# A fused attention and two-layer MoE kernel: ScalarE's gate moved one copy later, K and Q asked for two units ahead

## The chip, the cores and the metric

The kernel runs on one core of a Trainium2 chip. The metric is the device time of one execution in microseconds (us). The kernel before took 1169.15 us (median of 3 runs, 1167.33 to 1169.43).

## What is computed

Attention with a learned relative bias feeds two MLPs, all in float32, for 4 batches, 8 heads, 576 positions, 64 channels per head:

```python
x = (log1p(|i - j|) / log1p(max(i, 1)))[..., None]
bias = relu(x @ w1 + b1) @ w2                      # 576 x 576 for each of 8 heads
attn = softmax(q k^T / 8 + bias) @ v               # 4 x 8 x 576 x 64
x = attn.transpose(0, 2, 1, 3).reshape(2304, 512)
x = (sigmoid(x @ w_gate) * (x @ w_val)) @ w_out    # 512 -> 1536 -> 512
h = x @ w_in                                       # 512 -> 2048
out = (h * clip(h + 3, 0, 6) / 6) @ w_out2         # 2048 -> 512
```

## The kernel before, in words

**Chunks.** The query positions are cut into five chunks of 128, 128, 128, 128 and 64. A chunk's attention is made in units: one batch and one pair of heads, 16 units for a full chunk. The MLPs of a chunk run as a block of 68 steps (`STEPS`), and while block k runs, the attention of chunk k+1 is made between its steps.

**The lead** (`with ExitStack() as lead`, to line 584) makes the bias of chunk 0 and its 16 units. In turn n of its loop ScalarE takes the exponentials of unit n (L257) and the copies of unit n-1's transposes (L286), TensorE makes the product with V of unit n-2 (L302), and `att_x` splits it: ScalarE copies it to `xyh` (L321), VectorE puts the remainder into `xyl` (L322). The products with V take their PSUM banks from a pool of four, which the transposes share.

**Block 0** (`block(0)`) also prepares the weights. For each of the steps 2 to 67 SP loads the packed weight (`w_load`, L393, four buffers `wd`), `w_split` cuts it into a high and a low part (ScalarE L437, VectorE L438, L439, L442, ScalarE L447, VectorE L448, six buffers `wp`), and SP stores both parts for the later blocks (`w_store`, L453). A step is 12 products (L467): 4 slices of 128 rows, each high-high, high-low and low-high. The sum of a V step is taken out of PSUM by VectorE (L498). Early in block 0 the bias of chunk 1 is made as well, in three groups: hidden values z (ScalarE L125, VectorE L127), TensorE products (L136), ScalarE copies `bo` (L152), one store by SP (L162). Slice c of a block's input is ready when the units of head pair c have passed `att_x`; the last unit of chunk 0 is the last to do so for slice 3.

**What sets the order.** In the lead the orders of TensorE, ScalarE, VectorE and SP are written by hand. In block 0 those of TensorE and SP are; ScalarE's and VectorE's are laid out beforehand by a planner that goes by its own estimates, and each engine then works strictly in its order. Work of block 0 may be planned into the gaps of the lead, but two gates hold part of it: every SP instruction traced after the lead stands behind `gate`, every ScalarE instruction behind `gate_act` (lines 595, 596). `gate_act` is whatever `issued[1]` held at line 584: the last ScalarE instruction so recorded.

**Chunk 1's loads.** `chunk_att(1, 15.5, 67, 2)` (line 674) lays its events over block 0, one unit about every 3 steps. The event of a unit (`first`) asks for the bias rows and Q (`load_rows`, only with the first unit of a head pair) and K (`load_k`) of the next unit, then makes its own scores. K has four buffers, Q two, the bias rows two.

Of the kernel before, what the change touches and what calls it, by code (L numbers as in the profile page):

```python
# [12 lines left out]
AF = mybir.ActivationFunctionType  # L13
# [43 lines left out]
def fused_kernel(ctx: ExitStack, tc: tile.TileContext, qd, kd, vd, tz, rd, zc, w2b, iden, wpack, out):  # L57
    nc = tc.nc
# [22 lines left out]
    def mm_ps():  # L81
        return m1.tile([128, 512], F32, name="ps")
# [12 lines left out]
    t0 = S - QC[0][1]  # L95
# [10 lines left out]
    for g in (2, 3):  # L106
        nc.tensor.matmul(
            out=ps[32 * g:32 * g + 32, 0:2], lhsT=w2b_t, rhs=zc_t[:, 0:2], start=True, stop=True,
# [9 lines left out]
    def bias_hidden(G, g):  # L118

        if g == 0:  # L120
            z_q[G] = z_p.tile([128, 4, S], F32, name="z")
        t = 4 * G + g
        z, x = z_q[G][:, g], tz_t[:, S - 4 - 4 * t:2 * S - 4 - 4 * t]
        if g < 2:
            nc.scalar.activation(out=z, in_=x, func=AF.Relu, scale=sc_t[:, t:t + 1], bias=b1c)  # L125
        else:
            nc.vector.tensor_scalar(  # L127
                out=z, in0=x, scalar1=sc_t[:, t:t + 1], scalar2=zc_t[:, 2:3], op0=ALU.mult, op1=ALU.max
            )

    def bias_mm(G):
        z = z_q.pop(G)
        ps = bo_q[G] = s_ps()
        for j in range(2):
            for g in range(4):
                nc.tensor.matmul(  # L136
                    out=ps[32 * g:32 * g + 32, j, 0:NI], lhsT=w2b_t, rhs=z[:, g, NI * j:NI * j + NI],
                    start=True, stop=True, tile_position=(0, 32 * g),
                )
# [28 lines left out]
    xs, bm_q, q_q, kv_q, st, issued = {}, {}, {}, {}, {}, {}  # L168

    def bias_read(u):  # L170
        c, hp, b = u
        n = QC[c][1]
        if b == 0:
            bm = bm_p.tile([128, 2, S], F32, name="bm")
            for p in range(0, NQ, n):
                nc.sync.dma_start(out=bm[p:p + n], in_=biasD[c][:, 2 * hp:2 * hp + 2, :])
            bm_q[c, hp] = bm

    def load_rows(u, bias=True):
        c, hp, b = u  # L180
        i0, n = QC[c]
        if bias:
            bias_read(u)
        if b == 0:
            qt = q_p.tile([128, B, NQ], F32, name="qt")
            nc.sync.dma_start(out=qt[:, :, 0:n], in_=qd[hp, :, :, i0:i0 + n])
            q_q[c, hp] = qt

    def load_k(u):
        c, hp, b = u  # L190
        kts = []
        for a in range(NQ // QC[c][1]):
            kts.append(A["k"].tile([128, S], F32, name="kt"))
            nc.sync.dma_start(out=kts[a], in_=kd[b + a, hp])
        kv_q[u] = [kts, None]

    def load_v(u):
        c, hp, b = u
        vts = kv_q[u][1] = []
        for a in range(NQ // QC[c][1]):  # L200
            vts.append(A["v"].tile([128, 10, D], F32, name="vt"))
            issued[0] = nc.sync.dma_start(out=vts[a], in_=vd[b + a, hp])

    def att_load(u, bias=True):
        load_rows(u, bias)
        load_k(u)
        load_v(u)
# [14 lines left out]
    def att_qk(u):  # L222

        c, hp, b = u
        n = QC[c][1]
        kts, qt = kv_q[u][0], q_q[c, hp]
        ps = [s_ps(), s_ps()]
        for j in range(2):
            for h in range(2):
                for a, kt in enumerate(kts):  # L230
                    r = slice(64 * h, 64 * h + 64)
                    nc.tensor.matmul(  # L232
                        out=ps[h][n * a:n * a + n, j, 0:NI], lhsT=qt[r, b + a, 0:n],
                        rhs=kt[r, NI * j:NI * j + NI], start=True, stop=True, tile_position=(64 * h, n * a % 128),
                    )
        st[u] = dict(ps=ps)
# [37 lines left out]
    def att_tr(u, part, mm_ps):  # L274

        d = st[u]
        if part == 0:
            d["pt"] = pt_p.tile([128, 9, NQ], F32, name="pT")
        p = d["s"].rearrange("p h j -> p (h j)")
        ps = mm_ps()  # L280
        for t in range(3):
            k = 3 * part + t
            nc.tensor.transpose(  # L283
                out=ps[:, t * NQ:t * NQ + NQ], in_=p[:, 128 * k:128 * k + 128], identity=id_t
            )
        issued[1] = nc.scalar.activation(  # L286
            out=d["pt"][:, 3 * part:3 * part + 3],
            in_=ps[:, 0:3 * NQ].rearrange("p (t n) -> p t n", t=3), func=AF.Copy,
        )
# [17 lines left out]
    def att_x(u, po=None):  # L307

        c, hp, b = u
        n = QC[c][1]  # L310
        w = NQ if po is None else 2 * NQ
        d = st.pop(u)
        if po is None:
            po = d["po"]
        if (c, hp) not in xs:
            xs[c, hp] = (
                xy_p.tile([128, NTOK], F32R, name="xyh"),
                xy_p.tile([128, NTOK], F32R, name="xyl"),
            )
        xh, xl = (x[:, b * n:b * n + w] for x in xs[c, hp])  # L320
        nc.scalar.activation(out=xh, in_=po[:, 0:w], func=AF.Copy)  # L321
        nc.vector.tensor_tensor(out=xl, in0=po[:, 0:w], in1=xh.bitcast(F32), op=ALU.subtract)  # L322


# [54 lines left out]
    def pair_av(p):  # L379
        po = mm_ps()  # L380
        for i, u in enumerate(p):
            att_av(u, lambda: po[:, NQ * i:NQ * i + NQ])
        att_x(p[0], po)
        del st[p[1]]
# [148 lines left out]
    us = units[0]  # L533
    NL = len(us)
    NG0, NG1 = QC[0][1] // 16, 2
    with ExitStack() as lead:
        for name, bufs in (("s", 3), ("k", 6), ("v", 7), ("bo", 3), ("wf", 2), ("cv", 2)):
            A[name] = lead.enter_context(tc.tile_pool(name=name + "l", bufs=bufs))
        lead.enter_context(tc.manual_schedule(engines={ET.PE, ET.Activation, ET.DVE, ET.SP}))
        load_rows(us[0], False)  # L540
        load_k(us[0])
        nc.sync.dma_start(out=tz_t[:, 0:t0], in_=tz[:, 0:t0])
        load_k(us[1])
        load_v(us[0])
        nc.sync.dma_start(out=id_t, in_=iden)
        load_k(us[2])
        bm_q[0, 0] = bm_p.tile([128, 2, S], F32, name="bm")
        for G in range(NG0 + NG1 + 1):
            if G < NG0 + NG1:
                for g in range(4):  # L550
                    bias_hidden(G, g)
                bias_mm(G)
            if G:
                bias_out(G - 1, (G - 1) % 2, G % 2 == 0)
        for u in us[1:3]:
            load_v(u)
        att_qk(us[0])
        att_min(us[0])
        att_qk(us[1])
        for n in range(NL + 2):  # L560
            if n + 3 < NL:
                att_load(us[n + 3])
            if n in (1, 6):
                w_load(n // 6)
            if n < NL:
                att_exp(us[n])
            if n + 1 < NL:
                att_min(us[n + 1])
            if 1 <= n <= NL:
                for part in range(3):  # L570
                    att_tr(us[n - 1], part, mm_ps)
            if n < NL:
                att_norm(us[n])
            if n >= 2:
                att_av(us[n - 2], mm_ps)
                att_x(us[n - 2])
            if n + 2 < NL:
                att_qk(us[n + 2])
            if 4 <= n < 16:
                w_part((n - 4) // 6, (n - 4) % 6)  # L580
            if n == NL - 4:
                gate = issued[0]
            if n == NL - 1:
                gate_act = issued[1]

    def late(name, bufs):
# [29 lines left out]
    def chunk_att(c, t0, t1, lag):  # L616

        us = units[c]
        d = (t1 - t0) / (len(us) - 1 + lag)
        ev = [(t0 - 2 * d, lambda: att_load(us[0], False)), (t0 - d, lambda: bias_read(us[0]))]  # L620
        for i, u in enumerate(us):
            a = t0 + d * i

            def first(u=u, nxt=us[i + 1] if i + 1 < len(us) else None):
                if nxt:
                    load_rows(nxt)
                    load_k(nxt)
                att_qk(u)
                att_min(u)
                att_exp(u)  # L630
                att_norm(u)
            if i:
                ev.append((a + 0.5, lambda u=u: load_v(u)))
            for part in range(3):
                ev.append((a + lag * d - 3 + part, lambda u=u, p=part: att_tr(u, p, mm_ps)))
            ev.append((a + lag * d - 0.01, lambda u=u: (att_av(u, mm_ps), att_x(u))))
            ev.append((a, first))
        return ev
# [136 lines left out]
```

## Time and profile before

| | |
|---|---|
| median of 3 runs | 1169.15 us (1167.33 to 1169.43) |
| profiled execution, its own time | 1166.04 us |
| its span in the profile | 1164.2 us |
| TensorE busy with matmuls | 1143.6 us (98%) |
| VectorE, ScalarE busy | 631.8 us (54%), 579.7 us (50%) |
| mean granted TensorE clock | 0.996 |

The profile names engines PE (TensorE), DVE (VectorE), ACT (ScalarE) and SPq (SyncE's queue, which issues the DMAs). Times run from the start of the span. In a timeline a bracket at the end of a row gives the idle time of the engine before the row and what ended it. A granted clock of 1.00 is 2.4 GHz, and 0.50 is 1.2 GHz.

### The profile page before, as it was taken

The page shows a single profiled execution, that of the slowest core. Times are in us where ns is not written, and L with a number is a line of the kernel's source. Part 1 is how long each engine was busy: PE and PEld are TensorE (multiplying, and loading weights), DVE is VectorE, ACT ScalarE, POOL GpSimd, SP SyncE. Part 2 cuts the span into 40 slices and gives each one's busy share as a digit, 9 for nine tenths or more (in the row PEclk, how much of TensorE's full clock was granted, in tenths as well). Part 3 has the DMA queues.
Part 4 walks back from the last instruction along what each step waited for, and adds up shares of the span by engine and source line. Part 5 has one row for each costly group of instructions (what it writes and reads, how often), then busy time and mean ns, then how long its engine had stood idle before and what let it go on. Part 6 is the DMA issues. An engine that isn't in the chain of part 4 may idle for free.

```text
span 1164.2 us, 20307 instructions
## 1 busy us (share of the span) xinstructions
PE 1143.6 (98%) x7676; PEld 926.2 (80%) x7676; DVE 631.8 (54%) x1496; ACT 579.7 (50%) x1162; POOL 0.2 (0%) x4
## 2 busy tenths in 40 slices
PE   7989989999999999999999999999999999999998
PEld 3767667777777788878888787888878888889998
DVE  6897899898853544684534543544332424232232
ACT  7786778788853434675534443444222224231231
POOL 0000000000000000000000000000000000000000
PEclk9999999999999999999999999999999999999999
DMA  6946999999968666676586656565685866557997
GB/s 208 352 170 237 353 388 391 361 349 368 348 207 290 211 227 226 197 238 223 187 264 198 213 190 231 189 219 194 206 269 181 273 205 215 196 194 254 364 368 272
DMA packets 115345, 297.65 MB, mean 256 GB/s; under 512 B 20400, under 2 KB 35120, under 8 KB 115248
## 3 DMA queue, kind: packets, MB, share of 16 engines
q1 hardware_dynamic: 114816, 296.27, 73.5%
q8 instruction: 61, 1.00, 0.3%
q14 instruction: 36, 0.29, 0.1%
q10 hardware_dynamic: 432, 0.09, 0.0%
HBM read 244.73 MB, written 50.99 MB: 254 GB/s over the span
## 4 chain that ended last, share of the span: by engine, by line
PE 92%; DMA 3%; DVE 2%; ACT 2%; issue 1%; SPq 0%; ACTq 0%
PE ps L467 69%; PE ps L302 7%; PE ps L283 6%; PE ps L136 3%; PE ps L232 3%; PE ps L343 2%; DMA wd<-wpack 1%; PE ps L349 1%; ACT z L125 1%; DMA wsp<-wp 1%; DMA kt<-kd 0%; DMA w2b_t<-w2b 0%; DVE cm L442 0%; ACT bo L152 0%; DVE wp L448 0%
## 5 line engine op out<-in xcount | busy, mean ns | idle before, releaser
L467 PE MATMUL ps<-xyh,wp 128*128 128x512 f32 (+1 forms) x1600 | 478.6, 375 | 2.0 <-DVE wp L448 1.0
L467 PE MATMUL ps<-gh,wp 128*128 128x512 f32 (+1 forms) x1120 | 343.4, 377 | 0.0
L467 PEld LDWEIGHTS ps<-xyh,wp 128*128 128x128 f32 x1600 | 291.0, 189 | 60.3 <-issue 4.1
L467 PE MATMUL ps<-xyl,wp 128*128 128x512 f32 (+1 forms) x800 | 295.5, 369 | 0.0
L467 PEld LDWEIGHTS ps<-gh,wp 128*128 128x128 f32 x1120 | 203.5, 189 | 36.0 <-issue 1.9
L467 PE MATMUL ps<-gl,wp 128*128 128x512 f32 (+1 forms) x560 | 206.7, 369 | 0.0
L467 PEld LDWEIGHTS ps<-xyl,wp 128*128 128x128 f32 x800 | 151.4, 189 | 22.5
L286 ACT ACTIVATE pT<-ps 128x384 f32<-128x384 f32 x216 | 100.3, 488 | 121.5 <-PE ps L283 121.4
L476 ACT ACTIVATE gh<-tmp 128x512 fp32r<-128x512 f32 (+1 forms) x140 | 82.4, 589 | 111.7 <-DVE tmp L498 75.1
L478 DVE TENSOR_TENSOR gl<-tmp,gh 128x512 fp32r<-128x512 f32 (+1 forms) x140 | 89.2, 637 | 66.7 <-ACT gh L476 66.5
L257 ACT ACTIVATE s<-s,m 128x576 f32<-128x576 f32 x144 | 110.4, 769 | 25.0 <-DVE m L365 16.1
L467 PEld LDWEIGHTS ps<-gl,wp 128*128 128x128 f32 x560 | 106.0, 189 | 14.9
L283 PEld LDWEIGHTS ps<-id_t,s 128*128 128x128 f32 x648 | 78.2, 140 | 31.8 <-issue 7.8
L283 PE MATMUL ps<-id_t,s 128*128 128x128 f32 x648 | 100.6, 275 | 0.5 <-DVE s L270 0.4
L498 DVE SCALAR_TENSOR_TENSOR tmp<-tmp,ps 128x512 f32<-128x512 f32 (+1 forms) x60 | 38.0, 633 | 111.8 <-PE ps L467 110.6
L302 PE MATMUL ps<-pT,vt 128*64 128x128 f32 (+1 forms) x1600 | 93.3, 269 | 3.6 <-DVE xyl L322 3.6
L302 PEld LDWEIGHTS ps<-pT,vt 128*64 128x64 f32 x1600 | 80.7, 139 | 19.2 <-issue 11.3
L504 DVE SCALAR_TENSOR_TENSOR tmp<-tmp,ps 128x512 f32<-128x512 f32 (+1 forms) x80 | 50.6, 633 | 68.9 <-ACT tmp L503 67.2
L503 ACT ACTIVATE tmp<-ps 128x512 f32<-128x512 f32 (+1 forms) x80 | 44.2, 552 | 48.9 <-PE ps L467 47.3
L494 ACT ACTIVATE tmp<-ps 128x512 f32<-128x512 f32 (+1 forms) x60 | 33.2, 553 | 66.9 <-PE ps L467 66.8
L322 DVE TENSOR_TENSOR xyl<-ps,xyh 128x128 fp32r<-128x128 f32 (+1 forms) x52 | 17.7, 341 | 86.3 <-ACT xyh L321 86.0
L125 ACT ACTIVATE z<-tz_t,zc_t,sc_t 128x576 f32<-128x576 f32 x72 | 57.1, 861 | 5.7 <-PE ps L136 3.1
(58 smaller groups left out, 944.6 us busy)
## 6 DMA issues: line engine op xcount, KB each, us to landing
wp<-wsp SPq DMA_DIRECT2D x272, 512.0 KB, 4.2
wd<-wpack SPq DMA_DIRECT2D x68, 512.0 KB, 6.9
wsp<-wp SPq DMA_DIRECT2D x68, 512.0 KB, 6.4
vt<-vd SPq DMA_DIRECT2D x80, 320.0 KB, 4.8
kt<-kd SPq DMA_DIRECT2D x80, 288.0 KB, 5.3
biasD<-bo SPq DMA_DIRECT2D x18, 576.0 KB, 3.2
bm<-biasD SPq DMA_DIRECT2D x15, 576.0 KB, 5.1
qt<-qd SPq DMA_DIRECT2D x16, 256.0 KB, 6.6
```

The costliest lines, as they stand in the source:

```text
L125: nc.scalar.activation(out=z, in_=x, func=AF.Relu, scale=sc_t[:, t:t + 1], bias=b1c)
L136: nc.tensor.matmul(out=ps[32 * g:32 * g + 32, j, 0:NI], lhsT=w2b_t, rhs=z[:, g, NI * j:NI * j + NI], start=True, stop=True, tile_position= ...
L257: nc.scalar.activation(out=s[:, h], in_=s[:, h], func=AF.Exp, scale=-1.0, bias=d["m"][:, h:h + 1], accum_out=r[:, h:h + 1],)
L283: nc.tensor.transpose(out=ps[:, t * NQ:t * NQ + NQ], in_=p[:, 128 * k:128 * k + 128], identity=id_t)
L286: issued[1] = nc.scalar.activation(out=d["pt"][:, 3 * part:3 * part + 3], in_=ps[:, 0:3 * NQ].rearrange("p (t n) -> p t n", t=3), func=AF. ...
L302: nc.tensor.matmul(out=po[64 * h:64 * h + 64, n * a:n * a + n], lhsT=vt[:, v], rhs=pt[:, k, n * a:n * a + n], start=(t == 0), stop=(t == 4 ...
L467: nc.tensor.matmul(out=ps[:, 0:nt], lhsT=w[:, c, :], rhs=x[:, 0:nt], start=(first and c == 0 and i == 0), stop=(last and c == 3 and i == 2),)
L476: nc.scalar.activation(out=hi[:, 0:nt], in_=src, func=AF.Copy, scale=scale)
L478: nc.vector.tensor_tensor(out=lo[:, 0:nt], in0=src, in1=hi[:, 0:nt].bitcast(F32), op=ALU.subtract)
L498: nc.vector.scalar_tensor_tensor(out=th, in0=th, scalar=1.0, in1=ps, op0=ALU.add, op1=ALU.mult)
L503: nc.scalar.activation(out=t, in_=ps, func=AF.Relu, bias=3.0)
L504: nc.vector.scalar_tensor_tensor(out=t, in0=t, scalar=6.0, in1=ps, op0=ALU.min, op1=ALU.mult)
```

## The change

`gate_act` is now the copy of an attention output (L321), not the copy of transposes (L286), and it is taken one turn later (n = 16): that is the `att_x` of unit 14, the last but one. In `chunk_att` the event of unit i now asks for K, Q and bias rows of unit i+2, and those of unit 1 are asked for one unit's time before unit 0's event.

```diff
-        issued[1] = nc.scalar.activation(
+        nc.scalar.activation(
             out=d["pt"][:, 3 * part:3 * part + 3],
...
-        nc.scalar.activation(out=xh, in_=po[:, 0:w], func=AF.Copy)
+        issued[1] = nc.scalar.activation(out=xh, in_=po[:, 0:w], func=AF.Copy)
...
-            if n == NL - 1:
+            if n == NL:
                 gate_act = issued[1]
...
-        ev = [(t0 - 2 * d, lambda: att_load(us[0], False)), (t0 - d, lambda: bias_read(us[0]))]
+        ev = [
+            (t0 - 2 * d, lambda: att_load(us[0], False)),
+            (t0 - d, lambda: (bias_read(us[0]), load_rows(us[1]), load_k(us[1]))),
+        ]
...
-            def first(u=u, nxt=us[i + 1] if i + 1 < len(us) else None):
+            def first(u=u, nxt=us[i + 2] if i + 2 < len(us) else None):
                 if nxt:
                     load_rows(nxt)
                     load_k(nxt)
```

## Rows read from the trace of the kernel before

**Rows 1.** The page, busy time of the engines: share of the span, instructions

```profile
PE 1143.6 (98%) x7676; PEld 926.2 (80%) x7676; DVE 631.8 (54%) x1496; ACT 579.7 (50%) x1162; POOL 0.2 (0%) x4
```

**Rows 2.** TensorE's waits from 70 to 350 us: total, times, longest

```profile
PE ps L302 <- DVE xyl L322: 3.6, 1, 3.6
PE ps L232 <- DMA kt<-kd: 2.3, 1, 2.3
PE ps L467 <- DVE wp L448: 1.0, 2, 0.5
PE ps L467 <- DVE tmp L498: 0.9, 1, 0.9
```

**Rows 3.** Windows: length, PE, PEld, DVE, ACT, POOL busy, clock, DMA, GB/s

```profile
87.00:93.00 6.00, 6.00 (x44) 4.75 (x44) 5.05 (x10) 3.79 (x8) 0.00 (x0) 0.56 0.85 283
...
156.00:163.00 7.00, 6.31 (x27) 4.77 (x28) 6.17 (x13) 3.84 (x8) 0.00 (x0) 0.76 1.02 390
150.00:167.00 17.00, 13.83 (x61) 10.43 (x59) 15.73 (x35) 13.16 (x26) 0.00 (x0) 0.90 1.02 399
...
350.00:1164.00 814.00, 809.74 (x5423) 674.84 (x5421) 337.16 (x849) 313.97 (x628) 0.00 (x0) 1.00 0.69 232
```

**Rows 4.** Timeline of ScalarE where the lead ends: start, length, engine, line, operation

```profile
82.09 1.29 ACT L437 ACTIVATE cm<-wd 128x512 f32<-128x512 f32 x2
83.23 3.16 ACT L125 ACTIVATE z<-tz_t,zc_t,sc_t 128x576 f32<-128x576 f32 x4
86.26 0.30 ACT L321 ACTIVATE xyh<-ps 128x128 fp32r<-128x128 f32 x1
```

**Rows 5.** Timeline of TensorE there

```profile
77.92 1.31 PE L302 MATMUL ps<-pT,vt 128*64 128x128 f32 x20
...
86.94 3.67 PE L302 MATMUL ps<-pT,vt 128*64 128x128 f32 x30 [3.58 <-DVE xyl L322]
```

**Rows 6.** Timeline of VectorE from the end of the lead to the first bias group

```profile
88.25 1.29 DVE L448 TENSOR_TENSOR wp<-cm,wp 128x512 fp32r<-128x512 f32 x2 [0.77 <-ACT wp L447]
...
102.44 1.29 DVE L442 SCALAR_TENSOR_TENSOR cm<-wd,cm 128x512 uint32<-128x512 uint32 x2
...
107.37 1.07 DVE L127 TENSOR_SCALAR z<-tz_t,sc_t,zc_t 128x576 f32<-128x576 f32 x2 [0.91 <-PE ps L136]
```

**Rows 7.** Timeline of ScalarE up to the first bias copy

```profile
103.16 1.28 ACT L447 ACTIVATE wp<-cm 128x512 fp32r<-128x512 f32 x2 [1.76 <-DMA wsp<-wp]
...
107.37 0.74 ACT L152 ACTIVATE bo<-ps,cv_t 128x576 f32<-128x576 f32 x1 [0.54 <-PE ps L136]
```

**Rows 8.** Timeline of SP's queue: the bias store and the weight load behind it

```profile
110.28 0.37 SPq L162 DMA_DIRECT2D biasD<-bo  x1
110.70 0.47 SPq L393 DMA_DIRECT2D wd<-wpack  x1
```

**Rows 9.** Timeline of ScalarE: the load's arrival, and the last copy of the second bias group

```profile
116.66 0.69 ACT L437 ACTIVATE cm<-wd 128x512 f32<-128x512 f32 x1 [2.10 <-DMA wd<-wpack]
...
122.94 0.72 ACT L152 ACTIVATE bo<-ps,cv_t 128x576 f32<-128x576 f32 x1
...
130.42 0.66 ACT L437 ACTIVATE cm<-wd 128x512 f32<-128x512 f32 x1 [3.17 <-DMA wd<-wpack]
```

**Rows 10.** Timeline of TensorE at step 14, the first short wait for a weight

```profile
138.77 0.73 PE L467 MATMUL ps<-xyh,wp 128*128 128x512 f32 x2 [0.54 <-DVE wp L448]
```

**Rows 11.** Timeline of SP's queue: unit 0's bias rows, unit 1's K

```profile
140.45 0.32 SPq L176 DMA_DIRECT2D bm<-biasD  x1
...
147.60 0.49 SPq L194 DMA_DIRECT2D kt<-kd  x1
```

**Rows 12.** Timeline of TensorE: unit 1's scores, and step 21

```profile
156.69 1.91 PE L232 MATMUL ps<-kt,qt 64*128 64x288 f32 x8 [2.34 <-DMA kt<-kd]
...
167.06 0.50 PE L467 MATMUL ps<-xyh,wp 128*128 128x512 f32 x1 [0.89 <-DVE tmp L498]
```

**Rows 13.** Timeline of VectorE: step 19's sum taken out of PSUM

```profile
166.32 0.68 DVE L498 SCALAR_TENSOR_TENSOR tmp<-tmp,ps 128x512 f32<-128x512 f32 x1
```

## The prediction, made before the run

> **What bounds the kernel now.** I read the page first: TensorE is busy 98% of the span [rows 1], so a change pays only where TensorE stands still or runs slowly, and whatever is won must last to the end. TensorE's waits come next: between 70 and 350 us it stands still in a handful of places, and two of them are what the change is aimed at, 3.6 us for `xyl` and 2.3 us for a K transfer [rows 2]. After 350 us it is busy 809.74 of 814 us at full clock [rows 3]; nothing is to be had there. The windows show that each of the two waits costs more than its length, since the granted clock falls to its lower level about it: 0.56 on average over 6 us after the first, 0.76 over 7 us at the second, which is 6 x 0.44 = 2.6 us and 7 x 0.24 = 1.7 us of work lost [rows 3]. The two places together hold 3.6 + 2.6 = 6.2 us and 2.3 + 1.7 = 4.0 us, 10.2 in all. That is the most that the change can bring. Whether it arrives is decided by block 0's first twenty steps, and there the timelines of the other engines are to be read, since a TensorE that is earlier can still find the next thing late.
>
> **Part 1, the gate.** What it removes: ScalarE, once past the gate at 82.1, takes two splits of weights (1.29 us) and four z (3.16 us), and only then, at 86.26, the copy of unit 13 [rows 4]. Unit 14's product needs that PSUM bank and starts at 86.94 after 3.58 us [rows 5]. With the new gate the copy of unit 13 goes ahead of all this, TensorE goes on where it stopped, at 86.94 - 3.58 = 83.4, and two products with V of 1.31 us [rows 5] are done at 86.0. So TensorE gains up to 6.2 us here.
>
> What it adds: the gate opens behind unit 14's copy, at 83.4 + 1.3 + 0.3 = 85.0 (an estimate from the same rows), 2.9 us later than before. Behind it the queue is the same, and unit 15's copy is not protected: the planner may again put splits and z before it. That delays slice 3 of the first step by nothing (copy at once) up to 1.29 + 3.16 us (all six before it), less the work on slices 0 to 2 that TensorE has meanwhile. Bounds 0 and 3; I take 1.0, as TensorE needs a share of the time in which the planner fills. Left: 5.2 us ahead.
>
> What is late next. The weights of steps 2 onwards start 2.9 us later. VectorE had 0.77 us of idle before their last operation [rows 6] and no longer has the two remainders of units 14 and 15 among them, which I count as 0.6 together; so it is about 1.5 late at 88.25, and from there to 107.37 it has no idle piece of that length, only 0.91 at the end, where it waited for TensorE [rows 6]. ScalarE is tied to it: its two L447 at 103.16 need VectorE's L442 pair, which ends at 103.7, and the first bias copy, at 107.37, stands behind them in a strict order. That copy had waited for TensorE for just 0.54 us [rows 6, 7]. TensorE five us earlier can therefore bring it forward by 0.54 at most; the late splits can push it back by 1.5 - 0.9 = 0.6. I take 0.
>
> From there a chain runs that TensorE has no part in. SP's queue is in order, and the store of the bias at 110.28 waits for that group's copies; the weight load of step 11 stands behind the store, at 110.70 [rows 8]. ScalarE waits for its arrival (116.66), makes the second group's copies behind it (122.94), the next store lets the load of step 14 go, ScalarE waits for that too (130.42) [rows 9], and TensorE, in step 14, waits for the result at 138.77 even now [rows 10]. Its wait there is 0.54 us; a TensorE that comes 5.2 us earlier waits the 5.2 us longer, in front of steps 11 to 14. A low clock there costs nothing, since the weight is what is late. **Part 1: -6.2 + 1.0 + 5.2 = 0**, with bounds -6.2 (nothing late next) and +1.5 (the splits' delay lasts).
>
> **Part 2, K and Q.** No instruction is added. In SP's queue the fifteen K loads of units 1 to 15, three Q loads and three reads of bias rows move one unit's time forward, past the weight loads and stores of some three steps; V stays. Unit 1's K goes from 147.60 to behind the bias rows at 140.45 [rows 11]. At 147.60 it took until 156.7, some nine us, so it lands near 150, and the scores of unit 1 start at 154.35 without the wait [rows 12]. No move makes SP wait: three K of four buffers are then in use, and the Q and bias buffers that are asked for were left two units before. The DMA engines are full there (share 1.02 at 399 GB/s [rows 3]); a K of 128 x 576 x 4 bytes, 0.29 MB, ahead of the weights is 0.7 us at that rate. Bounds 0 and 0.7; I take 0, because the load that it delays is one that ScalarE reaches late anyway. Won: 2.3 + 1.7 = 4.0.
>
> What is late next is step 21. It needs the bank of step 19's sum, which VectorE takes out at 166.32, and TensorE waits 0.89 us for it now, at 167.06 [rows 12, 13]. VectorE is not late there by an accident: from 150 to 167 it is busy 15.73 of 17 us [rows 3], in a strict order in which this L498 has splits of later steps before it. So it can come at most 1.3 us earlier, and TensorE, 4.0 ahead, waits 4.9 instead of 0.9. I take 0.5 of the 1.3. And the low clock changes its place: now it lies before the wait at 167.06, which swallows it; then it follows a wait of nearly five us, and behind it no wait is left up to 350 [rows 2] that could swallow anything. Its price is between 0 (the wait falls into pieces) and 2.6 us (as after the first wait), the nearest row being the second wait's 1.7, which I take. **Part 2: -4.0 + 4.0 - 0.5 + 1.7 = +1.2**, bounds -4.0 and +3.3.
>
> **The sum.** The profiled execution took 1166.04 us (span 1164.2), so 1166.04 + 0 + 1.2 = 1167.2. It lies 3.1 below the median of the runs; on the median's footing that is 1170.3.
>
> **A rule weighed.** The rows say that TensorE is held by a chain of loads, splits and a full VectorE just behind both waits [rows 3, 9, 10]. The Trainium skill, in "Perfetto Trace Analysis", section "Optimization Strategies", says that where the matmul engine idles for other engines one should relieve the engine that blocks it; by that alone, both blockers being relieved, the whole 10.2 us come off. That is the first rival below.
>
> **The rivals.**
>
> *All of it is won.* The planner puts the bias copies and step 19's L498 further forward once ScalarE's start of the block lies elsewhere, and no weight is late. For it: the order on ScalarE and VectorE is planned anew. Against it: rows 6 and 13 show VectorE without idle, whatever the order. 1169.15 - 10.2 = 1159. Chance 0.07.
>
> *One of the two is won in part.* Either some 3 to 5 of the 5.2 us of part 1 last, because the first bias copy is planned before the two L447, or L498 moves before the later splits and part 2 keeps most of its 4.0. For it: one place in an order is enough. 1164 to 1166. Chance 0.20.
>
> *It is slower.* TensorE meets the nearly five us of waiting before step 21, and the low clock behind it lasts as long as after the first wait: +2.6. On top the K transfer in the full DMA stretch delays a weight by 0.7, and with it L498, and the later splits add 0.6: +3.9, or 1173. It decides as soon as the low clock behind step 21 costs more than about 2.3 us. For it: both long waits so far were followed by such a stretch [rows 3]. Against it: a wait in two pieces may cost less. Chance 0.17.
>
> *The change doesn't do what it says.* Unit 15's copy is planned behind all the z and a wait of 3 us stands at the block's start in place of the old one. Part 1's gain is then small from the start, nothing is given back, part 2 goes as above: 1169 to 1170. Chance 0.04.
>
> **How the numbers follow.** The forecast (both gains are given back within block 0) has the remaining 0.52, from 1168 to 1172. About 0.2%, or 2.3 us, is what a measurement of this kernel can tell from no change: 1166.8 to 1171.5. Of the forecast's chance 0.41 lies inside and 0.11 above. Faster: 0.07 + 0.20 = 0.27. Same: 0.41 + 0.04 = 0.45. Slower: 0.11 + 0.17 = 0.28. The likeliest single time is the sum, 1170.3. The range leaves out the full gain and the far edges of the partial and the slower case, 0.15 or so: 1164.0 to 1173.5; the forecast's own is 1168 to 1172.
>
> **What the profile of the changed kernel would show.** Right for part 1: no wait of 3.6 us near 87, ScalarE's two L437 at about 85 behind two copies L321, step 2 some five us earlier than before, then waits of TensorE for `wp` or for z between 120 and 140 that add up to some five us, and step 15 at its old time within 1.5 us. The store of the first bias group at its old 110 within one us. Right for part 2: unit 1's scores without a wait for K, and a wait of four to five us for L498 before step 21, with a granted clock under 1 after it. From step 22 on the same steps at the same times, or up to three us later. Wrong: step 15 five us earlier (then the chain of loads was not what binds, or the planner moved the bias copies), or step 21 four us earlier with L498 ahead of the splits; also a TensorE wait after 200 us, which I don't expect at all, since a new plan could put one there.

## The result, and the profile after

The changed kernel takes 1156.89 us (median of 5 runs, 1156.38 to 1157.77), beside 1167.33 us (5 runs, 1165.18 to 1169.43) for the kernel before on the same chip: a ratio of 0.991, 95% interval 0.9893 to 0.9928. The prediction was 1170.3 us, no change, with 1164.0 as its lower end. About the whole gain arrived: 1167.33 - 1156.89 = 10.4 us, where 10.2 had been named as the most. In a later and larger set of runs (`both_again`, below) it is 8.9 us, 1157.09 beside 1166.02 (21 runs of the kernel before). The profiled execution took 1156.42 us, its span is 1154.6 us.

The page of the changed kernel, busy time of the engines (compare [rows 1]), and TensorE's waits from 70 to 350 us (total, times, longest; compare [rows 2]):

```profile
PE 1139.8 (99%) x7676; PEld 923.2 (80%) x7676; DVE 630.9 (55%) x1496; ACT 579.7 (50%) x1162; POOL 0.2 (0%) x4
```

```profile
PE ps L467 <- DVE wp L448: 0.9, 1, 0.9
PE ps L467 <- ACT xyh L321: 0.8, 1, 0.8
PE ps L283 <- DVE s L270: 0.4, 1, 0.4
PE ps L467 <- ACT pT L286: 0.2, 1, 0.2
```

Both aimed-at waits are gone, and so is the wait for L498. TensorE's own work is 1143.6 - 1139.8 = 3.8 us shorter with the same 7676 instructions, since the low clock no longer falls on it (mean granted clock 0.999, before 0.996); the other 9.6 - 3.8 = 5.8 us of the span are waits. The windows say the same (length, busy time of PE, PEld, DVE, ACT, POOL, granted clock, DMA share, GB/s):

```profile
83.00:87.00 4.00, 4.00 (x48) 3.12 (x45) 2.92 (x7) 3.41 (x8) 0.00 (x0) 1.00 0.36 137
87.00:93.00 6.00, 5.24 (x23) 3.87 (x22) 4.90 (x11) 4.97 (x9) 0.00 (x0) 1.00 0.57 183
93.00:139.00 46.00, 46.00 (x271) 34.22 (x271) 43.37 (x79) 35.83 (x58) 0.00 (x0) 1.00 0.95 351
...
150.00:167.00 17.00, 17.00 (x101) 13.36 (x98) 16.78 (x38) 14.20 (x30) 0.00 (x0) 1.00 1.01 378
350.00:1154.00 804.00, 800.16 (x5380) 667.18 (x5378) 334.97 (x846) 312.44 (x626) 0.00 (x0) 1.00 0.69 231
```

The row to study is the third. The same stretch of the kernel before, which the prediction does not use:

```profile
93.00:139.00 46.00, 45.46 (x265) 33.98 (x265) 35.78 (x66) 32.58 (x53) 0.00 (x0) 1.00 0.76 281
```

VectorE had stood idle for 10.2 of 46 us and the DMA engines for a quarter of the time. The changed kernel does more there: VectorE 43.37 us, DMA share 0.95. The room for a TensorE five microseconds earlier was in the old trace, only not inside the 20 us that the prediction uses.

The front of block 0 after, ScalarE (start, length, engine, line, operation; a bracket gives the idle time before the row and what ended it), then TensorE:

```profile
84.63 0.28 ACT L321 ACTIVATE xyh<-ps 128x128 fp32r<-128x128 f32 x1 [0.59 <-PE ps L302]
84.81 1.23 ACT L437 ACTIVATE cm<-wd 128x512 f32<-128x512 f32 x2
85.94 3.13 ACT L125 ACTIVATE z<-tz_t,zc_t,sc_t 128x576 f32<-128x576 f32 x4
88.97 0.25 ACT L321 ACTIVATE xyh<-ps 128x128 fp32r<-128x128 f32 x1
...
102.41 0.74 ACT L152 ACTIVATE bo<-ps,cv_t 128x576 f32<-128x576 f32 x1 [0.54 <-PE ps L136]
```

```profile
83.27 1.96 PE L302 MATMUL ps<-pT,vt 128*64 128x128 f32 x30
...
89.27 0.50 PE L467 MATMUL ps<-xyh,wp 128*128 128x512 f32 x1 [0.76 <-ACT xyh L321]
```

Unit 14's copy comes at 84.63, the gate opens, and splits and z stand before unit 15's copy, which costs 0.76 us at 89.27. The first bias copy waits for TensorE for 0.54 us as before [rows 7], but five us earlier. SP's queue after (bias stores, unit 1's K), and VectorE's L498 of step 19 (before: 110.28 for the first store [rows 8], 147.60 for K [rows 11], 166.32 for L498 [rows 13]):

```profile
105.84 0.38 SPq L162 DMA_DIRECT2D biasD<-bo  x1
116.47 0.37 SPq L162 DMA_DIRECT2D biasD<-bo  x1
...
126.44 0.38 SPq L162 DMA_DIRECT2D biasD<-bo  x1
...
134.07 0.89 SPq L194 DMA_DIRECT2D kt<-kd  x1
```

```profile
153.80 0.69 DVE L498 SCALAR_TENSOR_TENSOR tmp<-tmp,ps 128x512 f32<-128x512 f32 x1
```

In the old trace the second and third store stood at 123.69 and 134.89. Counting TensorE's products, 12 to a step, gives the start of each step:

| step | before, us | after, us | difference |
|---|---|---|---|
| 2 | 97.9 | 92.9 | -5.0 |
| 13 | 134.7 | 129.7 | -5.0 |
| 15 | 141.2 | 135.6 | -5.6 |
| 19 | 159.1 | 150.6 | -8.5 |
| 21 | 167.1 | 156.8 | -10.2 |
| 22 | 173.0 | 162.5 | -10.5 |
| end of span | 1164.2 | 1154.6 | -9.6 |

Where did the forecast waits go? The order of ScalarE and VectorE is another one. For the first copy of each bias group, this is the last step whose split had been begun (L437) and whose high part had been made (L447) ahead of it on ScalarE:

| kernel | group 1 | group 2 | group 3 |
|---|---|---|---|
| before, and K alone | 10 / 9 | 12 / 10 | 14 / 13 |
| after, and the gate alone | 8 / 6 | 10 / 9 | 13 / 12 |

On VectorE, L498 of step 19 stood behind L442 of step 23 before, and stands behind that of step 21 after.

### The profile page after: what moved, and what is told of

Read it like the earlier page. It is cut to its first block, busy times and chain, and to the rows that moved or that the text cites. A ratio compares the mean times of both kernels' runs of the same rounds, so it can differ in the third digit from the quotient of the medians.

```text
span 1154.6 us, 20301 instructions
## 1 busy us (share of the span) xinstructions
PE 1139.8 (99%) x7676; PEld 923.2 (80%) x7676; DVE 630.9 (55%) x1496; ACT 579.7 (50%) x1162; POOL 0.2 (0%) x4
## 4 chain that ended last, share of the span: by engine, by line
PE 85%; DVE 5%; ACT 4%; DMA 3%; issue 2%; SPq 0%; ACTq 0%; DVEq 0%
PE ps L467 65%; PE ps L302 7%; PE ps L283 6%; PE ps L136 3%; PE ps L343 2%; PE ps L232 2%; DVE wp L448 1%; DMA wd<-wpack 1%; ACT cm L437 1%; DVE cm L442 1%; PE ps L349 1%; DVE cm L439 1%; ACT s L257 1%; ACT z L125 1%; DMA kt<-kd 1%
## 5 line engine op out<-in xcount | busy, mean ns | idle before, releaser
L467 PE MATMUL ps<-xyh,wp 128*128 128x512 f32 (+1 forms) x1600 | 478.1, 375 | 1.8 <-DVE wp L448 0.9
L467 PE MATMUL ps<-gh,wp 128*128 128x512 f32 (+1 forms) x1120 | 343.6, 378 | 0.2 <-ACT pT L286 0.2
L467 PEld LDWEIGHTS ps<-xyh,wp 128*128 128x128 f32 x1600 | 290.5, 189 | 59.5 <-issue 3.8
L467 PE MATMUL ps<-xyl,wp 128*128 128x512 f32 (+1 forms) x800 | 295.6, 369 | 0.0
L467 PEld LDWEIGHTS ps<-gh,wp 128*128 128x128 f32 x1120 | 203.6, 189 | 36.3 <-issue 2.1
L467 PE MATMUL ps<-gl,wp 128*128 128x512 f32 (+1 forms) x560 | 206.9, 369 | 0.0
L467 PEld LDWEIGHTS ps<-xyl,wp 128*128 128x128 f32 x800 | 151.3, 189 | 22.7 <-issue 0.2
L286 ACT ACTIVATE pT<-ps 128x384 f32<-128x384 f32 x216 | 100.2, 487 | 122.4 <-PE ps L283 122.1
L467 PEld LDWEIGHTS ps<-gl,wp 128*128 128x128 f32 x560 | 106.1, 189 | 14.8
L498 DVE SCALAR_TENSOR_TENSOR tmp<-tmp,ps 128x512 f32<-128x512 f32 (+1 forms) x60 | 38.0, 633 | 110.8 <-PE ps L467 110.2
L125 ACT ACTIVATE z<-tz_t,zc_t,sc_t 128x576 f32<-128x576 f32 x72 | 57.1, 857 | 5.5 <-PE ps L136 3.1
```

The lines of the kernel that those rows point to most:

```text
L286: nc.scalar.activation(out=d["pt"][:, 3 * part:3 * part + 3], in_=ps[:, 0:3 * NQ].rearrange("p (t n) -> p t n", t=3), func=AF.Copy,)
L467: nc.tensor.matmul(out=ps[:, 0:nt], lhsT=w[:, c, :], rhs=x[:, 0:nt], start=(first and c == 0 and i == 0), stop=(last and c == 3 and i == 2),)
L498: nc.vector.scalar_tensor_tensor(out=th, in0=th, scalar=1.0, in1=ps, op0=ALU.add, op1=ALU.mult)
```

## The experiments

**The two parts alone.** The gate without the K and Q part, and the K and Q part without the gate. Each undoes the other's lines of the diff:

```diff
# gate_only
-            (t0 - d, lambda: (bias_read(us[0]), load_rows(us[1]), load_k(us[1]))),
...
+        ev = [(t0 - 2 * d, lambda: att_load(us[0], False)), (t0 - d, lambda: bias_read(us[0]))]
...
-            def first(u=u, nxt=us[i + 2] if i + 2 < len(us) else None):
+            def first(u=u, nxt=us[i + 1] if i + 1 < len(us) else None):
# k_only
-            if n == NL:
+            if n == NL - 1:
```

(and in `k_only` the `issued[1]` goes back to the copy of the transposes.)

> The gate behind unit 14's copy alone, K asked for one unit ahead as before. Theory A (each part pays by itself, because a later gate and an earlier K each change the planned orders): the front gain of about 5.0 us stays, and a wait for unit 1's K stays, with the low clock about it, some 4 us: near 1161 us. Theory B (the gate's gain lasts only with the K asked for earlier, since the wait for VectorE before step 21 takes the rest): near 1166, with steps 22 on at the times of the kernel before.

Measured: 1157.73 us (1156.58 to 1159.37), ratio 0.9929 (0.9909 to 0.9948). Neither theory foresaw it. The gate alone brings nearly all: step 13 is 4.4 us ahead, step 21 8.7. The K wait vanished, though K keeps its old place in SP's order. TensorE and SP's queue in this run:

```profile
145.50 0.73 PE L467 MATMUL ps<-xyh,wp 128*128 128x512 f32 x2 [1.89 <-DVE wp L448]
...
150.72 1.24 PE L232 MATMUL ps<-kt,qt 64*128 64x288 f32 x8
```

```profile
145.85 0.42 SPq L194 DMA_DIRECT2D kt<-kd  x1
```

K was asked for at 145.85, and unit 1's scores begin at 150.72 without a wait, so the transfer took at most 4.9 us (4.4 by its landing, shown at the end); in the kernel before the same 288 KB took 9.0.

> K, Q and bias rows two units ahead alone, the gate as before. Theory A: VectorE's planned order has step 19's L498 right behind the splits of step 20 instead of those of step 23, so the wait for K goes without a new one: 4 to 5 us under the kernel before, near 1163. Theory B, the prediction's (VectorE is full there and step 21 waits whatever the order): 0 to 2 us over the kernel before, with a wait of 4 to 5 us for L498 before step 21.

Measured: 1161.6 us (1161.18 to 1163.13), ratio 0.9962 (0.9949 to 0.9975). Theory A: about 4.5 us, with the 3.6 us in front left as they were. L498 of step 19 moved forward by itself and no long wait before step 21 came. TensorE's waits from 70 to 350 us:

```profile
PE ps L302 <- DVE xyl L322: 3.6, 1, 3.6
PE ps L467 <- DVE wp L448: 0.7, 1, 0.7
```

The two parts are worth 8.4 and 4.5 us alone, and 10.4 together at most: they overlap. So the gate alone was run once more, beside the whole change.

> The new gate alone once more, with more rounds, beside the whole change. Theory A, K and Q two units ahead add something on top of the gate: the whole change is at least 0.6 us faster than this. Theory B, they add nothing once the gate stands where it does, since unit 1's K is already in time: the two medians lie within 0.6 us.

> The changed kernel unaltered, beside gate_again on the same chip. Theory A (K and Q add something): 1156 to 1157, at least 0.6 us below gate_again. Theory B (they add nothing): within 0.6 us of gate_again.

Measured: 1156.59 us (1155.63 to 1157.39), ratio 0.9922 (0.9908 to 0.9936), for the gate alone, and 1157.09 us (1155.77 to 1157.97), ratio 0.9926 (0.9912 to 0.994), for both. Theory B: with the gate in its new place, asking for K and Q earlier adds nothing that can be measured.

**The order of the bias copies.** The changed kernel, with one copy of the first group held behind L447 of step 9 (`bo_behind`), then with the copies of all three groups held at their old places (`bo_chain`), then, besides, with ScalarE's z of the next chunk behind the third group's copies and L447 of step 14 behind those z, as it was (`chain_z`). Some splits are traced earlier in the program so that there is something to stand behind; TensorE's and SP's orders stay.

```diff
# bo_chain; bo_behind has one entry: G == 10 behind ("hi", 9)
+BEHIND = {10: (("hi", 9), ("lo", 10)), 11: (("hi", 9), ("lo", 10)), 12: (("hi", 10), ("lo", 12)),
+          13: (("hi", 11),), 14: (("hi", 13), ("lo", 14)), 15: (("hi", 13), ("lo", 14))}
...
+            with ExitStack() as behind:
+                for w in BEHIND.get(G, ()):
+                    behind.enter_context(tc.issue_after(marks[w].ins))
+                nc.scalar.activation(out=bv, ...)
# chain_z, besides
+            with tc.issue_after(marks["bo", G - 2].ins) if G in (16, 17) else ExitStack():
+                marks["z", G] = nc.scalar.activation(out=z, ...)
+        with tc.issue_after(marks["z", 17].ins) if n == 14 else ExitStack():
+            marks["hi", n] = nc.scalar.activation(out=wv[:, 0], in_=f, func=AF.Copy)
```

> The changed kernel, with one copy of the first bias group held behind ScalarE's second part of the split of step 9, where it stood in the kernel before. Theory A (the place in the order decides): the store of the bias and the weight load behind it come at about 111 instead of 105.8, TensorE waits 3 to 5 us for weights in steps 11 to 14: 1160 to 1162. Theory B (the order of these copies does not matter, the splits' own pace does): within 1 us of the changed kernel, 1156 to 1158.

Measured: 1159.8 us (1159.43 to 1160.5), ratio 0.9945 (0.9931 to 0.996): one copy held back costs some 3 us (`l498_behind`, below, took 1156.51 in the same set of runs), just under theory A's 1160. TensorE's waits for weights from 70 to 350 us (its L449 is L448, L448 is L447, L468 is L467):

```profile
PE ps L468 <- DVE wp L449: 2.2, 4, 1.1
PE ps L468 <- ACT wp L448: 0.8, 2, 0.6
```

They lie in steps 13 (1.2 us), 17, 19 (1.1 us) and 21. The prediction had its chain's waits in front of steps 11 to 14, so this is that chain in part, with a smaller size, and later waits besides.

> The changed kernel, with the ScalarE copies of all three bias groups held behind the splits that stood ahead of them in the kernel before (the second part of step 9 and the first of step 10 for the first group, 11 and 12, 13 and 14 for the others). Theory A (the place of these copies makes the prediction's chain of loads): nearly all of the front gain is given back; TensorE waits 4 to 6 us for weights in steps 11 to 17, step 18 comes within 1.5 us of its time in the kernel before; what the K part holds alone stays: 1160.5 to 1163. Theory B (the later splits, not these copies, keep the gain): not over 1160, as with one copy held (1159.8).

Measured: 1159.39 us (1158.76 to 1161.39), ratio 0.9943 (0.9928 to 0.9958). All three groups held cost no more than the first; theory A, nearly all given back, is not borne out. (The profiled execution, at 1161.39, was the slowest of the four.) The load of step 14 left at about its old time less 1.5 us, but its split then ran through in 6 us, where in the kernel before two pairs of z lay inside it (L437 at 130.42 [rows 9], L447 at 136.82). That is what the next run adds.

> The changed kernel with all three groups' bias copies held at their old places (as in bo_chain) and, besides, ScalarE's four z of the next chunk held behind the third group's copies and L447 of step 14 held behind those z, as ScalarE had it before (131.98 to 137.3). Theory A, the prediction's chain binds, but only in the old order: the four z (3.2 us) now lie between the first and the last operation of step 14's split; L448 of step 14 ends near 137 instead of 134.0, TensorE waits some 3 us more before step 14 or 15, step 15 starts within 2.5 us of its old time, and the median is 1161 to 1163. Theory B, the chain of stores and loads does not bind even then: the planner or a spare weight takes it up, step 15 is still some four us early, median 1159 to 1160, as bo_chain.

Measured: 1162.9 us (1160.9 to 1164.56, 10 runs), ratio 0.9973 (0.9962 to 0.9984): theory A. It is 5.8 us over the whole change in the same set of runs (1157.09), and its interval overlaps that of K alone (0.9949 to 0.9975), a kernel without the gate: with the old order of the copies and of these z, what the gate adds to K alone can no longer be told from nothing. ScalarE and TensorE of this kernel (its L129 is L125, L463 is L447, L483 is L467):

```profile
129.67 3.14 ACT L129 ACTIVATE z<-tz_t,zc_t,sc_t 128x576 f32<-128x576 f32 x4
...
134.26 0.62 ACT L463 ACTIVATE wp<-cm 128x512 fp32r<-128x512 f32 x1
```

```profile
134.93 0.50 PE L483 MATMUL ps<-xyh,wp 128*128 128x512 f32 x1 [2.74 <-ACT wp L463]
```

The four z stand before the high part of step 14, and TensorE waits 2.74 us for it. Steps 2 to 13 are 5.4 us ahead of the kernel before, step 15 only 3.0. From step 13 to step 22 this kernel takes 37.5 us, the changed one 32.7 and the kernel before 38.3; of the 4.7 us lost, 3.0 are lost by step 15 and the rest in later steps. The profiled execution was the fastest of the ten, at a mean clock of 0.999; of the others some had clocks down to 0.995 (1164.49 us), which this trace does not show.

**The place of L498.** L498 of step 19 is held behind L442 of step 23, where the kernel before had it, once in the changed kernel (`l498_behind`) and once in the kernel with K and Q alone (`k_l498`):

```diff
+        marks["or", n] = nc.vector.scalar_tensor_tensor(   # L442
...
+            with tc.issue_after(marks["or", 23].ins) if n == 19 else ExitStack():
+                moe_step(k, i, P, mm_ps)
```

> The changed kernel, with step 19's sum taken out of PSUM behind VectorE's L442 of step 23, where it stood in the kernel before. Theory A: L498 comes at 159 to 160 instead of 153.8, step 21 waits 3 to 4 us for its bank and runs slowly behind it: 1160 to 1162. Theory B (VectorE has room enough to make it up, or step 21 is not held by that bank): 1156 to 1158.

Measured: 1156.51 us (1156.07 to 1158.24), ratio 0.9919 (0.9903 to 0.9935): theory B. L498 came at 158.40 instead of 153.80, and nothing waited for it.

> K and Q two units ahead alone (old gate, as k_only), with step 19's sum L498 held behind L442 of step 23 on VectorE, where it stood before. Theory A, the prediction's part 2 was right for the old order: L498 of step 19 comes near 163 to 166, step 21 waits 2 to 4 us for its bank, and of the 4.4 us that k_only won at most 2 remain: 1164 to 1166. Theory B, step 21 no longer takes the bank of step 19 (as in l498_behind): no such wait, 1161 to 1162, as k_only.

Measured: 1163.05 us (1159.92 to 1164.15, 10 runs), ratio 0.9972 (0.9961 to 0.9983). The median lies between the theories' ranges; the trace decides for B. VectorE:

```profile
161.16 0.69 DVE L442 SCALAR_TENSOR_TENSOR cm<-wd,cm 128x512 uint32<-128x512 uint32 x1
164.26 0.68 DVE L442 SCALAR_TENSOR_TENSOR cm<-wd,cm 128x512 uint32<-128x512 uint32 x1
164.86 1.28 DVE L498 SCALAR_TENSOR_TENSOR tmp<-tmp,ps 128x512 f32<-128x512 f32 x2
```

L498 of step 19 is as late as I had feared, 164.86, and step 21 had begun near 161 without a wait. So step 21 no longer takes the bank that step 19 filled: not only the orders, the PSUM banks too had been dealt out anew. The median is 1.5 us longer than `k_only`'s; the intervals overlap, and the span of the profiled execution (1159.7 us) is that of `k_only` (1159.8). Part of it goes with the granted clock: the two executions at a mean of 0.999 took 1159.92 and 1161.48 us, the two at 0.994 took 1163.86 and 1164.15. The rest stays open.

**What the gate must hold, and where.** Two kernels in which only the z, or only the splits, stand behind unit 14's copy (everything else at the old gate), and one with the gate behind the last unit:

```diff
# z_held: the old gate; and L125 behind unit 14's copy
+            with tc.issue_after(held[0].ins) if 0 in held else ExitStack():
+                nc.scalar.activation(out=z, ...)
# split_held: the old gate; and L437 behind unit 14's copy
+        with tc.issue_after(held[0].ins):
+            nc.scalar.activation(out=f, in_=high.bitcast(F32), func=AF.Copy, scale=2.0 ** -112)
# gate_x15
-            if n == NL:
+            if n == NL + 1:
```

> The changed kernel, but only the hidden values z of ScalarE wait behind unit 14's copy; the splits of weights may start at the old gate, 2.9 us earlier. The bias copies then stand 1 split later in the order than in the changed kernel, and 1 earlier than in the kernel before. Theory A (order): TensorE waits up to 1.2 us for unit 13's copy, which has two splits before it, little else: 1156.5 to 1159. Theory B (the gain needs the splits to be late): 1160 or more, with waits for weights near steps 13 to 18.

Measured: 1157.3 us (1154.99 to 1157.78), ratio 0.9918 (0.9903 to 0.9933): theory A, as the whole change.

> The changed kernel, but only the first operation of each split waits behind unit 14's copy; z may run at the old gate, ahead of unit 13's copy. Orders of splits and bias copies are about those of the changed kernel. Theory A: the front wait stays (four z of 3.16 us ahead of unit 13's copy: a wait of 2 to 3.5 us and the low clock behind it, 4 to 6 us together) and nothing later takes it back, so 1161 to 1163. Theory B (a later TensorE meets weights that are ready, and what is lost at the front is won where the changed kernel waits): 1158 to 1160.

Measured: 1159.43 us (1158.52 to 1161.36), ratio 0.9942 (0.9928 to 0.9957), in theory B's range. With the splits held but the z free, ScalarE puts the four z before unit 13's copy, and TensorE waits 2.4 us for it. Waits from 70 to 350 us, and the windows about the first of them:

```profile
PE ps L302 <- DVE xyl L322: 2.4, 1, 2.4
PE ps L468 <- DVE wp L449: 1.8, 3, 1.1
```

```profile
83.00:87.00 4.00, 1.59 (x26) 1.35 (x26) 0.89 (x2) 3.52 (x7) 0.00 (x0) 1.00 0.03 6
87.00:93.00 6.00, 6.00 (x41) 4.63 (x38) 4.45 (x10) 3.58 (x8) 0.00 (x0) 1.00 0.50 188
```

The z are thus the part that the gate must hold to win all; the splits held alone still win 6.7 us over the kernel before (1166.16 us in this set), though the z run at the old gate. In the profiled execution, the fastest of the four, the clock stayed up after this wait, so there it cost its length alone. The two slower executions, 1160.0 and 1161.36 us, had mean clocks of 0.998 and 0.997, and where it fell in them no trace shows.

> The changed kernel with the gate behind the copy of the last unit, 15. It takes away the 0.76 us for which TensorE waits for that copy in the changed kernel; the splits start about 1 us later still, where TensorE is 2.4 us behind them at step 2. Theory A: 1156 to 1157, less by up to 0.8. Theory B (the weights are now what is late): waits for weights in steps 2 to 10, 1158 to 1160.

Measured: 1158.85 us (1158.72 to 1160.35), ratio 0.994 (0.9923 to 0.9956): theory B. The 0.8 us for `xyh` are gone, but TensorE waits 3.6 us for weights. One unit before the last is the better place of the two. No kernel that was run beats the changed one by more than the intervals allow.

## Why the prediction was wrong

**Right: the front of part 1.** The terms were -3.6 for the wait, -2.6 for the clock and +1.0 for a new wait for unit 15's copy: 5.2 us ahead. Measured: 5.0 ahead at step 2, with a new wait of 0.76 us. The splits behind the gate were to be 1.5 us late at VectorE's L448 of step 2; that pair began 1.5 us later than before (89.78 against 88.25 [rows 6]).

**Wrong, and the failed step: the +5.2 of part 1.** It rested on "the first bias copy, at 107.37, stands behind them in a strict order", from which it followed that it could come forward by 0.54 us at most, and "Behind it the queue is the same". The order is strict once laid, but it is laid anew for each kernel, and the table of orders shows that the gate alone changes it. With the new gate the first bias copy stands behind the high part of step 6, not of step 9, and it came at 102.41, the very 5.0 us earlier at which TensorE delivered. All three bias stores moved with it (by 4.4, 7.2 and 8.5 us), and with them the weight loads behind them, so no weight was late by more than 0.9 us. `bo_behind` and `chain_z` show that the chain is there in the old order, though smaller: put the order back, and 3 and then 5.8 us are lost, and in `chain_z` the longest wait, 2.74 us, stands before step 14, the step named. Not all of the loss lies there: later steps have their share in both. What failed is that rows of the old order were taken for the order after. One of them was also read too simply: the two L447 at 103.16 are tied to VectorE's L442, but rows 7 name the landing of a weight store (`wsp`) as what ended ScalarE's wait there, at about the time at which the first L442 ended.

**Wrong: "VectorE without idle, whatever the order".** That reason was to make the full gain unlikely. From 93 to 139 us VectorE had been busy for 35.78 of 46 us. The prediction used the 20 us in which it was nearly full and not the 30 behind them.

**Wrong: the +4.0, -0.5 and +1.7 of part 2.** The wait before step 21 never came: L498 of step 19, at 166.32 before, came at 153.80 after and at 158.95 in `k_only`, and where it was forced back, step 21 used another bank. The low clock behind that wait fell away with it. The -4.0 for K itself was near what K alone brings (4.5, in which other waits moved too: those for weights in steps 14 and 15, 1.0 us, and for L498, 0.9 us [rows 2], went, and one of 0.7 us in step 21 came). But it was counted on top of part 1, and it does not stand on top: with the gate alone K is in time as well. That part 2 as a sum was wrong hardly shows in the time, since the gate alone would have brought the same.

**The rivals.** The first one, all of it won because "the planner puts the bias copies and step 19's L498 further forward", is what happened, by that mechanism; it had been given a chance of 0.07. The rule weighed there, from the Trainium skill's "Perfetto Trace Analysis", section "Optimization Strategies", that one relieves the engine that blocks TensorE, stood for the full 10.2 us. The trace agrees: its span is 9.6 us shorter. The slower case did not come near: no long wait and no granted clock under 1.00 stand in the windows after.

Why the planner lays the splits later behind a later gate, so that the bias copies get ahead of them, was not tried; that it does, the table of orders shows.

## What to carry to other kernels

Where a planner lays out an engine's order, the order is a result of the change, not a given: price a stall both with the old order and with one in which the held work simply goes later, and give the second a real chance, above all where the blocking engine has idle time somewhere in the stretch. Before a gain is called "given back", look at the busy time of every engine over the whole way to the point where it is to be lost. And two waits on one chain are not two gains: run each part alone, for here the second part added nothing to the first.

## What the runs showed of the hardware

**The same transfer took 4.4 or 9.0 us, and what was asked for just before it differed.** Unit 1's K is 288 KB in all kernels. DMA issues in a short window around its request, of the kernel before and of `gate_only` (KB each, median us to landing):

```profile
wsp<-wp SPq DMA_DIRECT2D x1, 512.0 KB, 8.6
kt<-kd SPq DMA_DIRECT2D x1, 288.0 KB, 9.0
```

```profile
kt<-kd SPq DMA_DIRECT2D x1, 288.0 KB, 4.4
```

SP's queue differs: the kernel before had issued a store and a load within the two us ahead of K's request, and a store and a load in the three before that; `gate_only` had issued nothing between a load at 140.56 and a store at 145.47, right ahead of K. Two more runs fit: 7.8 us in the changed kernel, where 576 KB of bias rows were asked for 0.4 us ahead, and 4.7 us in `gate_again`, after a pause of 3.6 us broken by one store right ahead. No run changes this alone, so the cause is argued and not shown. The prediction had given K's landing time (9 us) to the transfer, not to what it stood behind.

**The same kind of wait was followed by a low clock or not.** After the 3.6 us wait in front the granted clock from 87 to 93 us was 0.56 on average in the kernel before [rows 3], 0.51 in `k_only` and 0.72 in `k_l498`. After the 2.3 us wait for K it was 0.76 over 7 us [rows 3]. But after 2.4 us in `split_held`, and about the 2.7 us in `chain_z`, it was 1.00:

```profile
131.00:139.00 8.00, 5.12 (x20) 3.04 (x18) 5.61 (x11) 6.31 (x11) 0.00 (x0) 1.00 1.05 414
```

And in `bo_chain`, where no wait from 70 us on is longer than 1.4 us, the clock fell all the same:

```profile
139.00:167.00 28.00, 25.40 (x125) 17.83 (x125) 25.77 (x52) 20.60 (x39) 0.00 (x0) 0.94 1.01 395
```

It is 0.72 there from 150 to 156 us, right behind the 1.42 us wait, which ended at 150.44. Executions of one kernel differ as well (`split_held`, 1.000 to 0.997 on average). What such a wait costs beside its length can't be read from its length alone, nor from one trace.
